# Moving the sequence-DFT stage of a gated FNet and feed-forward kernel between gate/up and the last feed-forward product, with the T sums of h made there

## The chip, the core and the metric

The kernel runs on one core of one Trainium2 chip, in fp32 results. The metric is the device time of one execution in microseconds (us): the kernel before takes 1018.36 us, the median of 3 runs between 1018.31 and 1018.51 us. Five engines work side by side and wait for each other through semaphores: TensorE (PE, matrix products), VectorE (DVE), ScalarE (ACT), GpSimd (POOL) and SyncE (SP). In this kernel POOL and SP do nothing but issue DMAs, SP mostly loads and POOL mostly stores. Each engine takes its instructions in the order in which they stand in its queue.

## What is computed

With S = 2048, D = 640 and F = 1728 the reference is, cut to what matters:

```
g = sigmoid((x * gate_w).sum(-1))                       # one gate per row
a = x @ dft_hid_re.T ;  b = x @ dft_hid_im.T
A = dft_seq_re @ a - dft_seq_im @ b                     # real part of a 2-D DFT
B = (gelu(x @ w_gate) * (x @ w_up)) @ w_down            # feed-forward
out = g * A + (1 - g) * B
```

The kernel takes the sequence DFT first (u = dft_seq @ x for the real and the imaginary matrix) and the hidden DFT after it, on the result.

## The kernel before, in words

**Precision.** Each fp32 operand is split into a high and a low part (`split`: `high` is a copy on ACT, `low` a subtraction on DVE), and each product is three PE instructions (`mm3`, lines 101 to 103). A product is one weight block of 128x128 against 512 columns.

**Seven products for eight.** All stages work on 2x2 blocks with seven products and sums of blocks. The sums of the left factor are called S, those of the right factor T.

**The stages, in the order of the program.**

1. *Gate/up*, a loop over 13 blocks of F (f = 0 to 12). It makes h = gelu(gate) * up in pairs of blocks. `keep` stores h's four blocks of a pair to DRAM (`hA[tp][k]`) and also four sums of them (`hT[tp][k]`), tp = 0, 1 being the halves of the rows and k = 0 to 5 the pairs. Small work that PE doesn't wait for (sums of weights, splits of the next operands) is put into a list, `fills`, from which some is taken after each product.
2. *Down*, 28 steps of `kseq`: h times w_down, from `hA`/`hT` and from w_down with its sums (`wsd`, made by `sum_wd` in gate/up). A step loads three steps ahead (`load_k`) and splits two steps ahead (`split_k`). The rows of h's first block, which F leaves over, have sums of their own (`hL`, by `sum_h0` and `sum_h0_narrow`). The result, times 1 - g, goes to `out`.
3. *C*, 64 steps of `cseq`: blocks of the sequence DFT's two matrices (`ct`, re and im, two halves j) times blocks of x. Eight steps with b = 0 (five pairs of products, 30 PE instructions; result banks X, Z, V, L, two each) and eight with b = 1 (four pairs, 24 instructions; banks Q, R, Y and again X) make one round; there are four rounds. In step i SP loads the DFT blocks of step i + 3 (tiles `cra`, `crb`, 512 KB each), and DVE and ACT split those of step i + 2 (`split_c`; for b = 1 DVE first makes four sums, `csa` and `csb`). x's own blocks are loaded, summed and split in the first steps (`fetch_xn`, `split_xa`, `split_xb`; some of it in the down stage) and stay in SBUF. At the end of b = 0 the eight banks are copied out so that b = 1 gets six of them; at the end of b = 1 the results are stored (`uA`) with their T sums (`uT`).
4. *U*, 20 steps of `useq`: u times the hidden DFT's matrices, times g, added onto `out` by accumulating DMAs. Its weights' sums (`wsu`) are made by `sum_wu` in the C stage.

The logits of the gate (ten of sixteen in gate/up, six in down) are a multiply-and-reduce on DVE of a loaded tile `xz` with the gate weights (`load_z`).

**What sets the order.** ACT and DVE run in the order in which the code issues their work (`in_order`). A scheduler orders SP's and POOL's DMAs and PE's products when the program is built. Large tiles come from one pool of 46 buffers of 512 KB (`slot`), 256 KB tiles from a pool of 14 (`mtile`), and weight pieces of 128 KB from a pool of 6 (`wsmall`); a load waits until the tile that had its buffer is done with.

The C stage's split has one special place, which both kernels have. In the last step of b = 0 (`held`), X is copied out first, then the DFT blocks of step i + 2 are split, and only then Z and L are copied out, all on ACT:

```
            for d in range(2):
                mm3(X[d], A(0, d), B[0], fst, lst)
            if held:
                for d in range(2):
                    sv["c11", d] = copy(X[d], f"s1{n}{d}")
                prepare()
```

Of the kernel before, what the change touches and what calls it, by code (L numbers as in the profile page):

```python
# [14 lines left out]
P = 128  # L15
# [10 lines left out]
XN_LOAD, XN_AT = [1, 5, 18, 22], [3, 7, 21, 24]  # L26
# [4 lines left out]
ZE_AT = [6, 8]  # L31
XB_DOWN = [17, 18]
XB_AT = [1, 3, 4, 5, 9, 10]
WU_AT = [4, 17, 19, 33, 35]
# [3 lines left out]
def kernel(  # L38
# [36 lines left out]
    def mtile(dt, name):  # L75
        return pool.tile([P, T], dt, tag="m", name=name, bufs=14)
# [157 lines left out]
    late_work, left_work, left_out = [], [], []  # L234

    def spare():
        for _, do in left_work:
            do()
        left_work.clear()
# [24 lines left out]
    def make_w(f):  # L264
# [96 lines left out]
        if kind == 1:  # L361
            if f > PAIRED:
                work = [(0, high_a), (0, neg_a), (84, across), (0, low_a), (56, across2), (0, high_q)]
                work += [(84, sums), (109, low_q), (84, sums2), (0, high_c), (56, diff_high), (0, spare), (0, diff_low), (122, low_c)]
# [88 lines left out]
    hid, todo = {}, deque()  # L453
# [74 lines left out]
    def gate_up(f, W, B, tp, s5, s1t, xs, s4):  # L528
# [69 lines left out]
        if not second:  # L598
            tt(s5, s2, s1, op=ALU.subtract)
            keep(hT[tp][k], 0, s5)  # L600
            hid[tp] = s2, s5
            yield
        h12, t1 = hid.pop(tp)

        def last_sums():
            tt(h12, s2, h12, op=ALU.subtract)  # L606
            keep(hT[tp][k], 2, h12)
            tt(t1, s2, t1, op=ALU.subtract)
            keep(hT[tp][k], 1, t1)

        def last_sum():
            tt(s5, s1, t1, op=ALU.subtract)
            keep(hT[tp][k], 3, s5)

        todo.extend([(122, last_sums), (61, last_sum)])
# [17 lines left out]
    def sum_wd(k):  # L633

        work = []

        def load():
            r, a21 = slot(F32, [P, 8, P], f"dr{k}"), wsmall(F32, f"da{k}")
            nc.sync.dma_start(r, wd[k, :, :8])
            nc.sync.dma_start(a21, wd[k, :, 8:])  # L640
            work.extend(do for _, do in sums_left(nc.sync, r[:, 0:2], r[:, 2:4], r[:, 6:8], a21, wsd[k]))

        def do():
            work.pop(0)()

        return [(0, load), (84, do), (84, do)]
# [20 lines left out]
    def sum_h0_narrow(tp):  # L667
# [13 lines left out]
        def second():  # L681
            tt(b21, b21, d2, op=ALU.add)
            left_out.append((hL[tp][:, 1], b21))

        return [(122, first), (61, second)]

    LEFT_AT = {2: lambda: [*sum_h0(0), *sum_h0(1)], 6: partial(sum_h0_narrow, 0), 12: partial(sum_h0_narrow, 1)}
# [74 lines left out]
    def split_xa(sp):  # L762
# [7 lines left out]
        sums_made.append(partial(split, h, l, r))  # L770
# [77 lines left out]

    def split_pieces(i):

        n = "{}{}{}".format(*kseq[i])
        r, raw = kraw.pop(i)
        names = ("A11", "A12", "e5", "S4")
        assert not kseq[i][1]
        B, W = [], {}

        def weights():
            h, l = slot(F32R, [P, 8, P], f"kh{n}"), slot(F32R, [P, 8, P], f"kl{n}")
            split(h, l, r)
            W.update({name: (at((h, l), 2 * q), at((h, l), 2 * q + 1)) for q, name in enumerate(names)})  # L860

        def right(q):
            v = hl(f"kb{n}{q}")
            split(*v, raw[q])
            B.extend([at(v, 0), at(v, 1)])

        ktile[i] = W, B
        return [(122, weights), (122, lambda: right(0)), (122, lambda: right(1))]
# [400 lines left out]
    with in_order(PE, ACT, DVE, POOL):  # L1269
        for f in range(1, NF):  # L1270
# [9 lines left out]
            if kind == 1:  # L1280
                lw, *w = sum_wd((f - PAIRED) // 2)
                if f == PAIRED:
                    lw[1]()
                    fills.extend(w)
# [3 lines left out]
            if f == NF - 1:  # L1288
                lw, *w = sum_wd(NK - 1)
                lw[1]()  # L1290
                fills.extend(w)
# [498 lines left out]
```

## Time and profile before

| | before |
|---|---|
| median of 3 runs | 1018.36 us |
| the profiled execution's own time | 1018.28 us |
| its span, first to last instruction | 1016.5 us |
| PE busy | 1012.4 us, 4489 instructions |
| DVE busy | 828.5 us (82%) |
| ACT busy | 486.0 us (48%) |
| POOL busy | 165.7 us (16%) |
| bytes moved by DMA | 265.74 MB, mean 261 GB/s |

Busy shares are averages over the stages. From the profile's timeline the stages lie at about 0 to 330 us (gate/up), 330 to 497 us (down), 497 to 890 us (C) and 890 us to the end (U). In the rows of the profile an instruction is named by line, engine, operation and its tiles, written before read.

### The profile page before, as it was taken

The page shows a single profiled execution, that of the slowest core. Times are in us where ns is not written, and L with a number is a line of the kernel's source. Part 1 is how long each engine was busy: PE and PEld are TensorE (multiplying, and loading weights), DVE is VectorE, ACT ScalarE, POOL GpSimd, SP SyncE. Part 2 cuts the span into 40 slices and gives each one's busy share as a digit, 9 for nine tenths or more (in the row PEclk, how much of TensorE's full clock was granted, in tenths as well). Part 3 has the DMA queues.
Part 4 walks back from the last instruction along what each step waited for, and adds up shares of the span by engine and source line. Part 5 has one row for each costly group of instructions (what it writes and reads, how often), then busy time and mean ns, then how long its engine had stood idle before and what let it go on. Part 6 is the DMA issues. An engine that isn't in the chain of part 4 may idle for free.

```text
span 1016.5 us, 13263 instructions
## 1 busy us (share of the span) xinstructions
PE 1012.4 (100%) x4489; PEld 836.4 (82%) x4489; DVE 828.5 (82%) x1164; ACT 486.0 (48%) x622; POOL 165.7 (16%) x295
## 2 busy tenths in 40 slices
PE   9999999999999999999999999999999999999998
PEld 7888888888888888888888888888888888888887
DVE  8887887977687989889888985888488869797796
ACT  6644434354545657457444443434344344455340
POOL 0221232323221200100001022102210200021112
PEclk9999999999999999999999999999999999999999
DMA  8557587968689999978865678658866868897856
GB/s 313 158 199 259 197 275 236 303 224 285 198 304 313 405 374 388 340 258 294 303 255 179 211 241 325 223 195 295 302 203 207 303 249 275 297 341 224 268 144 95
DMA packets 95988, 265.74 MB, mean 261 GB/s; under 512 B 12656, under 2 KB 26864, under 8 KB 95920
## 3 DMA queue, kind: packets, MB, share of 16 engines
q1 hardware_dynamic: 70368, 185.24, 53.4%
q0 software_dynamic: 25264, 79.46, 23.4%
q8 instruction: 35, 0.57, 0.2%
q14 instruction: 33, 0.27, 0.1%
q10 hardware_dynamic: 288, 0.20, 0.1%
HBM read 192.48 MB, written 70.27 MB: 258 GB/s over the span
## 4 chain that ended last, share of the span: by engine, by line
PE 99%; DMA 0%; ACT 0%; DVE 0%; ACTq 0%; issue 0%
PE pX L101 7%; PE pX L102 7%; PE pX L103 7%; PE pZ L101 5%; PE pZ L102 5%; PE pZ L103 5%; PE pL L102 3%; PE pL L101 3%; PE pL L103 3%; PE pV L102 2%; PE pV L101 2%; PE pV L103 2%; PE pQ L101 1%; PE pY L102 1%; PE pY L101 1%; PE pR L101 1%
## 5 line engine op out<-in xcount | busy, mean ns | idle before, releaser
L82 ACT ACTIVATE ch<-csa 128x1024 fp32r<-128x1024 f32 x32 | 34.0, 1063 | 79.0 <-DVE csa L797 77.6
L85 DVE TENSOR_TENSOR cl<-cra,ch 128x1024 fp32r<-128x1024 f32 x32 | 39.1, 1221 | 26.8 <-ACT ch L82 24.7
L82 ACT ACTIVATE ch<-cra 128x1024 fp32r<-128x1024 f32 x32 | 33.9, 1059 | 52.0 <-DVE cl L85 15.7
L85 DVE TENSOR_TENSOR cl<-crb,ch 128x1024 fp32r<-128x1024 f32 x32 | 39.1, 1221 | 14.3 <-ACT ch L82 14.3
L102 PE MATMUL pL<-cl,xah 128*128 128x512 f32 x128 | 49.8, 389 | 0.0
L103 PE MATMUL pL<-ch,xal 128*128 128x512 f32 x128 | 49.8, 389 | 0.0
L101 PE MATMUL pL<-ch,xah 128*128 128x512 f32 x128 | 49.6, 389 | 0.0
L422 POOL DMA_DIRECT2D hA<-s x48 | 26.1, 545 | 138.8 <-DVE s L589 119.3
L82 ACT ACTIVATE ch<-crb 128x1024 fp32r<-128x1024 f32 x32 | 33.8, 1056 | 29.6 <-PE pL L102 11.6
L85 DVE TENSOR_TENSOR cl<-csb,ch 128x1024 fp32r<-128x1024 f32 x32 | 39.2, 1224 | 3.7 <-ACT ch L82 2.3
L85 DVE TENSOR_TENSOR cl<-csa,ch 128x1024 fp32r<-128x1024 f32 x32 | 39.1, 1220 | 2.1 <-ACT ch L82 1.1
L82 ACT ACTIVATE ch<-csb 128x1024 fp32r<-128x1024 f32 x32 | 34.0, 1062 | 11.7 <-DVE csb L800 5.3
L148 ACT ACTIVATE s<-pX 128x512 f32<-128x512 f32 x41 | 24.3, 596 | 28.9 <-PE pX L103 28.4
L583 ACT ACTIVATE s<-s 128x512 f32<-128x512 f32 x24 | 15.2, 633 | 45.6 <-DVE s L582 45.6
L82 ACT ACTIVATE kh<-kw 128x1024 fp32r<-128x1024 f32 x24 | 25.5, 1063 | 15.6 <-DMA kw<-wsd 6.4
L578 DVE TENSOR_TENSOR s<-s,pX 128x512 f32<-128x512 f32 x24 | 16.4, 684 | 20.0 <-PE pX L103 20.0
L1437 POOL DMA_DIRECT2D uA<-c x8 | 4.3, 540 | 168.9 <-DVE c L1539 168.6
L85 DVE TENSOR_TENSOR kl<-kw,kh 128x1024 fp32r<-128x1024 f32 x24 | 29.2, 1217 | 1.9 <-ACT kh L82 1.0
L422 POOL DMA_DIRECT2D hT<-s x48 | 25.9, 540 | 18.6 <-DVE s L606 7.4
L959 POOL DMA_DIRECT2D out<-ks x12 | 6.5, 541 | 136.4 <-DVE ks L958 135.8
L564 ACT ACTIVATE s<-pZ 128x512 f32<-128x512 f32 x24 | 14.2, 595 | 29.4 <-PE pZ L103 24.1
L101 PEld LDWEIGHTS pL<-ch,xah 128*128 128x128 f32 x128 | 24.0, 188 | 5.0
(3655 smaller groups left out, 3484.8 us busy)
## 6 DMA issues: line engine op xcount, KB each, us to landing
cra<-in_ct SPq DMA_DIRECT2D x64, 512.0 KB, 4.3
crb<-in_ct SPq DMA_DIRECT2D x64, 512.0 KB, 4.9
hA<-s POOLq DMA_DIRECT2D x48, 256.0 KB, 5.5
hT<-s POOLq DMA_DIRECT2D x48, 256.0 KB, 5.0
kr<-hA SPq DMA_DIRECT2D x24, 512.0 KB, 7.3
kr<-hT SPq DMA_DIRECT2D x24, 512.0 KB, 6.9
ux<-uA SPq DMA_DIRECT2D x24, 512.0 KB, 5.9
ux<-uT SPq DMA_DIRECT2D x16, 512.0 KB, 6.6
```

The costliest lines, as they stand in the source:

```text
L82: nc.scalar.activation(hi, raw, AF.Copy)
L85: nc.vector.tensor_tensor(lo, raw, hi.bitcast(F32), op=ALU.subtract)
L101: nc.tensor.matmul(ps, lh, rh, start=first, stop=False, skip_group_check=True)
L102: nc.tensor.matmul(ps, lh, rl, start=False, stop=False, skip_group_check=True)
L103: nc.tensor.matmul(ps, ll, rh, start=False, stop=last, skip_group_check=True)
L148: nc.scalar.activation(m, src, AF.Copy)
L422: nc.gpsimd.dma_start(to[:, i], src)
L564: nc.scalar.activation(s5, Z, AF.Copy)
L578: tt(s5, s5, X, op=ALU.add)
L583: nc.scalar.activation(s2, s2, AF.Gelu_apprx_tanh)
L959: nc.gpsimd.dma_start(acc4[:, t] if tp and e == 4 else out[2 * tp + t, e], src)
L1437: nc.gpsimd.dma_start(to[:, i], src)
```

## The change

The C stage is moved from behind the down stage to behind gate/up; the down stage then stands between C and U. With it:

- h's T sums are no longer made in gate/up from h's tiles in SBUF. `sum_h(tp, k)` loads the four blocks of `hA[tp][k]` again (four loads of 256 KB), makes the four sums on DVE and stores them (four stores of 256 KB). It runs twelve times in the second to fourth rounds of the C stage: at steps 18, 19, 20 and 29 of the first of them (counted from the start of C), and 16 and 32 steps later.
- the sums of w_down (`sum_wd`) are made at steps 18 and 20 of these rounds, two a round, and stored from POOL's queue instead of SP's.
- ten logits are made in the C stage (`ZC_AT`), loaded in the step named and summed in the next.
- x's blocks, which were loaded and split in down and in C's first steps, are now loaded and split in gate/up's last block and C's first eight steps; six of the eight low parts come from an accumulating DMA instead of DVE (`by_dma`).
- of the five sums of the hidden DFT's weights, three stay in C at other steps and two move into down.
- `sum_h0_narrow` moves into down, the load of the hidden DFT's weights from C's last round to the seam between down and U, the sigmoid of the first gate half from gate/up to the start of down; `mtile` gets 15 buffers for 14.

The diff, cut to its core:

```
-XN_LOAD, XN_AT = [1, 5, 18, 22], [3, 7, 21, 24]
-XB_DOWN = [17, 18]
-XB_AT = [1, 3, 4, 5, 9, 10]
-WU_AT = [4, 17, 19, 33, 35]
+XB_AT = [0, 1, 2, 3, 4, 5, 6, 7]
+WU_AT, WU_DOWN = [18, 34, 50], [10, 17]
...
-        return pool.tile([P, T], dt, tag="m", name=name, bufs=14)
+        return pool.tile([P, T], dt, tag="m", name=name, bufs=15)
...
-        if not second:
-            tt(s5, s2, s1, op=ALU.subtract)
-            keep(hT[tp][k], 0, s5)
-            hid[tp] = s2, s5
-            yield
...
-        todo.extend([(122, last_sums), (61, last_sum)])
         yield
...
+        r, a21 = slot(F32, [P, 8, P], f"dr{k}"), wsmall(F32, f"da{k}")
+        nc.sync.dma_start(r, wd[k, :, :8])
+        nc.sync.dma_start(a21, wd[k, :, 8:])
+        return [do for _, do in sums_left(nc.gpsimd, r[:, 0:2], r[:, 2:4], r[:, 6:8], a21, wsd[k])]
+
+    def sum_h(tp, k):
+        b11, b12, b21, b22 = (mtile(F32, f"ht{tp}{k}{q}") for q in range(4))
+        for q, v in enumerate((b11, b12, b21, b22)):
+            nc.sync.dma_start(v, hA[tp][k][:, q])
...
+            tt(b11, b12, b11, op=ALU.subtract)
+            keep(hT[tp][k], 0, b11)
+            tt(b12, b22, b12, op=ALU.subtract)
+            keep(hT[tp][k], 2, b12)
+            tt(b22, b22, b11, op=ALU.subtract)
+            keep(hT[tp][k], 1, b22)
+            tt(b21, b21, b22, op=ALU.subtract)
+            keep(hT[tp][k], 3, b21)
...
+        def by_dma():
+            high(h, r)
+            negative(l, r)
+            left_of(l, r)
...
+    HT_AT, WD_AT, ZC_AT = {}, {}, [17, 22, 30, 33, 38, 46, 49, 53, 54, 62]
+    for g in range(3):
+        for q, r in enumerate((2, 3, 4, 13)):
+            HT_AT[16 * g + 16 + r] = q % 2, 2 * g + q // 2
+        for q in range(2):
+            WD_AT[16 * g + 18 + 2 * q] = 2 * g + q
...
+        ready, units = units, []
+        if i in HT_AT:
+            units += sum_h(*HT_AT[i])
+        if i in WD_AT:
+            units += sum_wd(WD_AT[i])
+        if i in ZC_AT:
+            (_, first), (_, total) = load_z(1)
+            first()
+            units.append(total)
...
         held = not b and sp == NP - 1
         if not held:
             prepare()
+        for do in ready:
+            do()
```

How the queues change at the seam from b = 0 to b = 1 of the second round (steps 22 to 26; the first number in a name, as in `cra24`, is the step). SP's queue, the loads of steps 23 to 26, before:

```order
L788 DMA cra23_5651<-in_ct 128x1024
L788 DMA crb23_5652<-in_ct 128x1024
L788 DMA cra24_5700<-in_ct 128x1024
L788 DMA crb24_5701<-in_ct 128x1024
L788 DMA cra25_5750<-in_ct 128x1024
L788 DMA crb25_5751<-in_ct 128x1024
L788 DMA cra26_5798<-in_ct 128x1024
L788 DMA crb26_5799<-in_ct 128x1024
```

and in the changed kernel, from the last load of an h block (`ht`) on; `dr` and `da` are the pieces of w_down for `sum_wd`, `ua` one for `sum_wu`, `xz` the tile of a logit:

```order
L620 DMA ht013_3982<-hA01_66 128x512
L611 DMA dr1_3987<-in_wd 128x1024
L612 DMA da4_5571<-in_wd 128x256
L777 DMA cra24_4037<-in_ct 128x1024
L777 DMA crb24_4038<-in_ct 128x1024
L686 DMA ua2_5585<-in_wu 128x256
L777 DMA cra25_4095<-in_ct 128x1024
L777 DMA crb25_4096<-in_ct 128x1024
L726 DMA xz1_4099<-in_xz 128x640
L612 DMA da5_5705<-in_wd 128x256
L777 DMA cra26_4145<-in_ct 128x1024
L777 DMA crb26_4146<-in_ct 128x1024
```

Between the DFT loads now stand other loads, among them `da4` and `da5`, which belong to the fourth round (steps 50 and 52): the scheduler put them here, and each takes a buffer of the pool of six that an earlier `da` has until its sums are stored.

DVE's queue in the held step 23, from the last low part of step 24 on, before:

```order
L85 TENSOR_TENSOR cl24_1_5765<-csb24_5757,ch24_1_5764 128x1024
L796 TENSOR_TENSOR csa25_5812<-cra25_5750 128x512
L797 TENSOR_TENSOR csa25_5812<-crb25_5751,cra25_5750 128x512
L799 TENSOR_TENSOR csb25_5815<-crb25_5751,csa25_5812 128x512
L800 TENSOR_TENSOR csb25_5815<-csb25_5815,crb25_5751 128x512
```

and in the changed kernel:

```order
L83 TENSOR_TENSOR cl24_1_4112<-csb24_4104,ch24_1_4111 128x1024
L730 ISA xz1_4099,z_63<-xz1_4099,gwb_64 128x640
L730 ISA z_63 128x1
L785 TENSOR_TENSOR csa25_4160<-cra25_4095 128x512
L786 TENSOR_TENSOR csa25_4160<-crb25_4096,cra25_4095 128x512
L788 TENSOR_TENSOR csb25_4163<-crb25_4096,csa25_4160 128x512
L789 TENSOR_TENSOR csb25_4163<-csb25_4163,crb25_4096 128x512
```

The logit's reduction, which needs the load of `xz1`, moved ahead of step 25's four sums. ACT's queue at this place has the same work in the same order in both kernels; in the changed one it reads (`s1` are the copies of X, `s3` those of Z):

```order
L146 ACTIVATE s1010_4156<-pX010_3758 128x512
L146 ACTIVATE s1011_4158<-pX011_3759 128x512
L80 ACTIVATE ch25_0_4166<-csa25_4160 128x1024
L80 ACTIVATE ch25_1_4170<-csb25_4163 128x1024
L146 ACTIVATE s3010_4198<-pZ010_3760 128x512
L146 ACTIVATE s3011_4200<-pZ011_3761 128x512
```

The copies of Z stand behind the high parts of step 25, which read the sums of DVE above.

More of the change, by code (lines that the diff above doesn't have):

```diff
@@ L232, in load_up @@
         return r
[L234 to L239, printed above, removed]
+    late_work, left_out = [], []
     def make_up(f, r):
@@ L1317 @@
             store_left()
[L1318 to L1325 removed]
+            if f == 2:
+                k = len(fills) // 2
+                rest = [fills.pop() for _ in range(len(fills) - k)]
+                fills.extend([*sum_h0(0), *sum_h0(1), *reversed(rest)])
+                state["all"] = sum(c for c, _ in fills)
             for _ in range(4):
@@ L1594 @@
         if after:
-            after.pop(0)()
+            late() if i == 0 else after.pop(0)()
         if i < ND:
             load_uw(1, i)
+            if i < 2:
+                split_uw(0, ND - 2 + i)
+            split_uw(1, i)
         fst, lst = p == 0, p == ND - 1
```

191 lines of the change are left out of this document (71 added, 120 removed).

## The prediction

> **What bounds the kernel now.** I read the page first: span, busy times, the DMA slices and the chain that ended last.
>
> ```profile
> span 1016.5 us, 13263 instructions
> ...
> PE 1012.4 (100%) x4489; PEld 836.4 (82%) x4489; DVE 828.5 (82%) x1164; ACT 486.0 (48%) x622; POOL 165.7 (16%) x295
> ...
> GB/s 313 158 199 259 197 275 236 303 224 285 198 304 313 405 374 388 340 258 294 303 255 179 211 241 325 223 195 295 302 203 207 303 249 275 297 341 224 268 144 95
> ...
> PE 99%; DMA 0%; ACT 0%; DVE 0%; ACTq 0%; issue 0%
> ```
>
> PE is busy for all but 4.1 us of the span (1016.5 - 1012.4), and the chain is PE alone. Next, PE's waits, the whole answer:
>
> ```profile
> PE idle L1059 <- PEq L1778: 0.8, 1, 0.8
> PE pg L101 <- ACT w0h L82: 0.2, 1, 0.2
> ```
>
> After the start PE never waits, so nothing that is taken off DVE, ACT or a queue can shorten the run. Since a matmul's record overlaps the next one's, I take its pace from starts: the first product of step 23 of the C stage and that of step 24.
>
> ```profile
> 644.55 0.39 PE L101 MATMUL pX<-ch,xah 128*128 128x512 f32 x1
> ...
> 651.35 0.39 PE L101 MATMUL pX<-ch,xbh 128*128 128x512 f32 x1
> ```
>
> 6.80 us for 30 instructions is 0.2267 us each, with no gap to close. The change issues the same number of matmuls on the same shapes, with the start and the end of the program as they were. So PE's 1012.4 us stay, and the question is only whether PE begins to wait. I therefore looked at what feeds it, stage by stage (columns: busy us of PE, its weight loads, DVE, ACT and POOL; granted clock, DMA share, GB/s).
>
> ```profile
> 25.00:330.00 305.00, 305.00 (x1345) 252.04 (x1344) 244.89 (x434) 144.12 (x227) 77.61 (x141) 1.00 0.74 246
> ...
> 597.30:651.30 54.00, 54.00 (x240) 44.72 (x239) 39.31 (x52) 20.80 (x27) 13.23 (x25) 1.00 0.80 279
> ```
>
> Gate/up (first row) has a full PE, so DVE's freed time gains nothing there. The second row is the eight b = 0 steps of C's second round, steps 16 to 23. They already have the DMA engines busy for 0.80 of the time, right where the change puts most of its transfers.
>
> **The change part by part.**
>
> *Gate/up gives up* 48 sums on DVE, here two of their four groups, with a sum of 256 columns below them:
>
> ```profile
> L599 DVE TENSOR_TENSOR s<-s,s 128x512 f32<-128x512 f32 x12 | 8.3, 692 | 0.4
> ...
> L606 DVE TENSOR_TENSOR s<-s,s 128x512 f32<-128x512 f32 x12 | 8.2, 683 | 0.0
> ...
> L768 DVE TENSOR_TENSOR xm<-xm 128x256 f32<-128x256 f32 x8 | 3.4, 425 | 0.3
> ```
>
> With the other two groups of twelve that is 33 us of DVE, the 48 stores of POOL, the w_down sums and ten logits. All of it lay beside a PE that was never idle: gain 0.
>
> *C's rounds two to four take it over.* Three of a round's four `sum_h` and both `sum_wd` fall into the eight b = 0 steps. Sizes of the transfers:
>
> ```profile
> hT<-s POOLq DMA_DIRECT2D x48, 256.0 KB, 5.0
> ...
> xz<-in_xz SPq DMA_DIRECT2D x16, 320.0 KB, 5.4
> dr<-in_wd SPq DMA_DIRECT2D x6, 512.0 KB, 6.1
> ur<-in_wu SPq DMA_DIRECT2D x10, 256.0 KB, 6.5
> wsd<-dr SPq DMA_DIRECT2D x18, 128.0 KB, 1.8
> wsu<-ur POOLq DMA_DIRECT2D x15, 128.0 KB, 3.5
> wneg<-ur POOLq DMA_DIRECT2D x6, 256.0 KB, 6.4
> ```
>
> Bytes of these steps before: 279 GB/s for 54.0 us, 15.07 MB. Out go the two `sum_wu` that stood at steps 17 and 19: twice three loads and four stores (0.655 + 0.524 MB) and one `wneg` of two stores (0.524), 2.88 MB. In come one `sum_wu` (1.18), three `sum_h` of four loads and four stores of 256 KB each (24 x 0.262 = 6.29), two `sum_wd` (2 x 1.18 = 2.36), two logit tiles (0.66), and two early small loads, `da4` and `ua2` (0.26): 22.9 MB. Over eight steps (8 x 6.80 = 54.4 us) that is 421 GB/s. What can the engines carry? Stretches where they were full:
>
> ```profile
> 606.00:622.00 16.00, 16.00 (x72) 13.25 (x71) 11.68 (x16) 3.44 (x4) 6.49 (x12) 1.00 1.03 378
> ...
> 807.00:813.00 6.00, 6.00 (x29) 4.95 (x28) 3.12 (x3) 1.38 (x2) 0.54 (x1) 1.00 1.03 418
> ...
> 334.00:406.00 72.00, 72.00 (x326) 59.10 (x325) 66.99 (x80) 47.61 (x54) 6.68 (x13) 1.00 1.02 389
> ...
> 384.00:396.00 12.00, 12.00 (x55) 9.94 (x54) 12.00 (x15) 10.34 (x11) 2.18 (x4) 1.00 1.03 404
> ```
>
> With a share of 1.02 to 1.04 the rate is 378 to 418 GB/s. The first row is the nearest case: the same stage, the start of the same round, with loads and stores mixed. I take 378; the other end is 418. So **these eight steps ask for more than the channel carries**, and a lag builds up.
>
> *Where the lag reaches PE.* Step 23 is the held step: Z's copies on ACT stand behind step 25's high parts, these behind DVE's four sums for step 25, and these now stand behind the logit's reduction, whose tile SP loads behind all else. The first product into Q waits for ACT. Before, at this place:
>
> ```profile
> 645.43 1.28 ACT L148 ACTIVATE s<-pX 128x512 f32<-128x512 f32 x2 [3.92 <-PE pX L103]
> 646.61 1.05 ACT L82 ACTIVATE ch<-csa 128x1024 fp32r<-128x1024 f32 x1
> 647.55 1.05 ACT L82 ACTIVATE ch<-csb 128x1024 fp32r<-128x1024 f32 x1
> 648.50 1.07 ACT L148 ACTIVATE s<-pZ 128x512 f32<-128x512 f32 x2
> ```
>
> ```profile
> 641.59 1.22 DVE L85 TENSOR_TENSOR cl<-csb,ch 128x1024 fp32r<-128x1024 f32 x1
> 644.53 0.69 DVE L796 TENSOR_TENSOR csa<-cra 128x512 f32<-128x512 f32 x1 [1.72 <-PE pL L102]
> ```
>
> From DVE's first sum (644.53) to the end of the first Z copy (648.50 + 0.6) are 4.57 us. The logit itself and its landing:
>
> ```profile
> L747 DVE CUSTOM_DVE_ANT_0 xz<-xz,gwb x16: 810/816/819, 148.6 to 438.5; 128x640 f32<-128x640 f32 x16
> ...
> DMA to landing us min/median/max: 3.6/5.4/8.8
> ```
>
> ```profile
> L747 DVE DVE_READ_ACCUMULATOR2_ANT z<- 128x1 f32 x16 | 1.3, 80 | 0.0
> ```
>
> Of the 22.9 MB, step 26's DFT blocks (1.05) and about 1.0 of stores come after the logit tile, so 20.9 MB go first: 55.3 us at 378 GB/s, counted from the start of step 16. The shortest landing, 3.6 us, less the tile's own transfer leaves 2.7 us behind the last byte. The tile is there at 55.3 + 2.7 - 54.4 = 3.6 us after step 24 should begin. Then 0.82 + 0.08 on DVE and 4.57 to the copy: 9.1 us. PE has six instructions of step 24 (X, 1.36 us) and then waits: **7.7 us**. At 404 GB/s the same sum gives 4.1, at 418 2.4. Rounds three and four repeat it (logits at steps 38 and 54): 3 x 7.7 = 23.1 us.
>
> *DVE* in the eight steps: 39.3 us busy before, plus 12 sums of h at 0.69, eight of w_down at 0.42 (256 columns), two logits at 0.9, less one `sum_wu` (1.7): 51.0 of 54.4 us. It is just hidden. Its lead was 8.5 us (641.59 + 1.22 against 651.35), and it has only 3.4 us in hand if loads make it idle.
>
> *The seams.* Gate/up's last block gets two splits of x and of DFT blocks (each three sums of 256 columns, 1.27 us, and three low parts of 1.22, in all 9.9) for three low parts (3.7): 6 us more of DVE beside 17.7 us of PE (78 matmuls). Before, PE waited there 0; bounds 0 and 2, I take 1. From C to down, the last round's stores meet the loads of three steps; before, the same stores met U's loads with no wait: bounds 0 and 3, I take 1. C's first eight steps carry five more x loads, the accumulating DMAs and no `sum_h`; bounds 0 and 2, I take 0, for less is asked of the channel than above. Down to U, the moved gate, `sum_h0_narrow` and `mtile`'s fifteenth buffer: 0, between -0.5 and 2; they lie beside products and the down stage loses x's work.
>
> Sum against the profiled execution's own 1018.28 us (span 1016.5 and 1.8 around it; 0.08 under the median): 1018.28 + 23.1 + 2 = **1043 us**.
>
> *A rule of the Trainium skill.* The rows above put a full channel at 378 to 418 GB/s. "DMA: Bandwidth & Descriptors", section "Where 436 GB/s comes from", names 435 GB/s as the ceiling of the ports and says that for transfers between HBM and SBUF the HBM side, about 358, binds. By 435 the wait would be 0.4 us a round and the time 1021; by 358 it would be 10.8 and the time 1053. This trace agrees with neither: 389 over 72 us is above the one, and no full stretch that I read reaches the other.
>
> **The rivals.**
>
> *The channel carries more (1025 to 1036).* At 418 GB/s, 3 x 2.4 = 7.2 us: 1025 without the seams; at 404, 12.3 and 2: 1033. For it: two of the four rows are above 400. Against it: the nearest row is the lowest, and the 418 lasted 6 us. (By the skill's 435 the far end is 1021.)
>
> *Not slower (1018 to 1020).* The lag vanishes before step 24 if the logit's tile is early enough: 47.6 us for 20.9 MB (54.4 + 1.36 - 2.7 - 5.5), so 439 GB/s, or 18.0 MB at 378. The mechanism is prefetch: if SP gets buffers early, some eleven of the 24 transfers of h leave the crowded steps. For it: 20% of those steps is idle channel today, and step 24's low parts had 8.5 us to spare. Against it: each `ht` load waits for a buffer of the pool of fifteen, which the end of a round fills.
>
> *SP held up by `da` and `ua` loads (1052 to 1062).* `da4` stands ahead of step 24's blocks and waits until an earlier `da` was summed and stored by POOL. If that store takes the longest landing of anything on `hT`, loads among them (12.1 us, below), rather than the 5.0 of its stores, the queue runs dry for up to 7.1 us; half of it in three rounds is 10.6 us: 1054. DVE with 3.4 us in hand couldn't make it up.
>
> ```profile
> L422 POOL DMA_DIRECT2D hT<-s x48: 539/539/548, 68.7 to 346.1; - x48
> ...
> DMA to landing us min/median/max: 2.4/6.0/12.1
> ```
>
> **How the numbers follow.** Forecast (1036 to 1052): 0.46. More channel (1020.4 to 1036): 0.22. SP held up (over 1052): 0.19. Not slower: 0.12, and 0.01 that PE's idle 4.1 us shrink by half. The range 1022 to 1058 leaves out the case of no change and the far ends of both, some 0.19. About 0.2%, 2 us, is what a measurement of this kernel can tell from no change. Faster 0.01, same 0.11, slower 0.88.
>
> **What would show it.** PE's waits in the profile after: three of 4 to 9 us, on the first product into Q at steps 24, 40 and 56, released by ACT; ACT's high parts there idle for DVE's sums, and the logit's reduction idle for its load. DMA share about 1.0 from step 16 to 24 of rounds two to four, near 378 GB/s. Gate/up's DVE about 50 us lighter and PE's busy time unchanged. It would be wrong if the share stays under 0.95 there, if the waits come at steps 18 to 22 instead (DVE the bound), or if PE waits mostly at a seam.

## The result, and the profile after

| | before | changed |
|---|---|---|
| median | 1018.39 us (4 runs, 1018.31 to 1018.51) | 1059.86 us (4 runs, 1057.12 to 1063.71) |
| ratio, 95% interval | | 1.041 (1.037 to 1.045) |
| the profiled execution's own time, span | 1018.28, 1016.5 us | 1058.28, 1056.5 us |

The changed kernel is slower by 41.5 us; 25 were forecast, and the time lies 1.9 us above the range. First the page of the changed kernel:

```profile
span 1056.5 us, 13360 instructions
...
PE 1024.0 (97%) x4489; PEld 839.9 (79%) x4489; DVE 823.8 (78%) x1158; ACT 487.9 (46%) x625; POOL 185.0 (18%) x327
...
PE 62%; issue 16%; DMA 16%; DVE 3%; POOL 2%; ACT 0%; SPq 0%; POOLq 0%; DVEq 0%
```

The chain was PE alone; now it runs through DMAs and queues. PE's busy time rose by 11.6 us at an unchanged number of products, so waits alone are not the whole story. PE's waits (us in total, times, longest):

```profile
PE pQ L99 <- ACT s L146: 13.9, 2, 7.4
PE pX L99 <- ACT ch L80: 6.3, 2, 6.0
PE pX L99 <- ACT s L146: 3.4, 3, 1.5
PE pX L101 <- DMA xal<-xn: 2.3, 2, 1.6
PE pX L100 <- DVE cl L83: 1.4, 4, 0.5
...
PE kZ L99 <- DVE ksa L985: 0.7, 1, 0.7
PE pL L99 <- DVE sa L1469: 0.5, 2, 0.2
```

But for 0.2 us at step 8, the first three lines are waits at steps 24, 40 and 56: 23.4 us. The three long ones, of the kind that was forecast, are 7.4, 6.5 and 6.0, 19.9 us together; in the other 3.4 us (third line) the first product of these steps waits for the copy of X. Next, the b = 0 and b = 1 halves of rounds two to four, each window from the first product of a half to that of the next (busy us of PE, weight loads, DVE, ACT, POOL; granted clock, DMA share, GB/s):

```profile
434.71:490.63 55.92, 54.57 (x241) 44.86 (x240) 42.85 (x62) 15.59 (x17) 20.01 (x37) 1.00 1.00 351
490.63:544.31 53.68, 45.99 (x193) 37.35 (x193) 43.44 (x55) 22.95 (x27) 4.87 (x9) 0.94 0.78 261
544.31:600.95 56.64, 54.86 (x241) 44.78 (x240) 45.07 (x65) 15.78 (x17) 20.54 (x38) 1.00 1.00 371
600.95:653.60 52.65, 45.91 (x193) 37.30 (x194) 43.18 (x55) 22.50 (x27) 4.32 (x8) 0.90 0.72 251
653.60:709.25 55.65, 54.86 (x242) 44.78 (x240) 44.98 (x65) 17.42 (x22) 21.45 (x40) 1.00 1.02 384
709.25:762.08 52.83, 46.52 (x192) 37.74 (x193) 48.91 (x63) 24.66 (x29) 4.49 (x9) 0.94 0.92 339
```

At the prediction's pace of 0.2267 us a round of 432 instructions takes 97.9 us. Here the three take 109.6, 109.3 and 108.5: 11.7, 11.4 and 10.6 us lost, **33.7** in all. The spans differ by 40.0, so 6.3 us lie elsewhere: 4.2 in C's first round, 1.1 in the down stage, the rest scattered. The b = 0 halves have a full channel (the core's 16 DMA engines together; share 1.00 to 1.02) at 351 to 384 GB/s. Most of the loss sits at the start of the b = 1 halves, and there the mean clock is below 1. The first of these places, on DVE, ACT and PE:

```profile
490.63 0.50 PE L99 MATMUL pX<-ch,xbh 128*128 128x512 f32 x1 [1.35 <-ACT s L146]
...
495.26 0.83 DVE L730 CUSTOM_DVE_ANT_0 xz<-xz,gwb 128x640 f32<-128x640 f32 x1 [3.91 <-DMA xz<-in_xz]
496.01 0.69 DVE L785 TENSOR_TENSOR csa<-cra 128x512 f32<-128x512 f32 x1
497.42 1.06 ACT L80 ACTIVATE ch<-csa 128x1024 fp32r<-128x1024 f32 x1 [6.35 <-DVE csa L786]
499.62 1.07 ACT L146 ACTIVATE s<-pZ 128x512 f32<-128x512 f32 x2
500.25 0.80 PE L99 MATMUL pQ<-ch,xbh 128*128 128x512 f32 x1 [7.42 <-ACT s L146]
```

It is the forecast's chain: logit's tile, reduction, sums, high part, Z's copy, and a wait of 7.42 us (7.7 forecast). What PE then does is seen in the clock (the column after POOL) around it:

```profile
488.00:493.00 5.00, 3.21 (x12) 1.78 (x10) 3.27 (x4) 2.74 (x4) 1.22 (x3) 1.00 1.02 391
493.00:497.00 4.00, 0.00 (x0) 0.00 (x0) 1.74 (x4) 0.00 (x0) 0.00 (x0) 1.00 0.38 137
497.00:498.00 1.00, 0.00 (x0) 0.00 (x0) 0.96 (x3) 0.58 (x1) 0.00 (x0) 0.58 0.95 283
...
500.00:503.00 3.00, 2.75 (x7) 2.17 (x8) 3.00 (x5) 1.66 (x4) 1.30 (x3) 0.50 0.99 356
...
504.00:506.00 2.00, 2.00 (x11) 1.60 (x9) 1.81 (x2) 1.38 (x2) 0.00 (x0) 1.00 0.72 169
```

The clock falls to half during the wait and stays there for 3.7 us after PE resumed: 7 products in 3 us, where 11 take 2 us later. And SP's queue ahead of this place, with what it waited for between 434 and 762 us:

```profile
467.01 0.33 SPq L611 DMA_DIRECT2D dr<-in_wd  x1
477.45 0.33 SPq L612 DMA_DIRECT2D da<-in_wd  x1
477.87 0.38 SPq L777 DMA_DIRECT2D cra<-in_ct  x1
478.67 0.33 SPq L777 DMA_DIRECT2D crb<-in_ct  x1
...
481.64 0.49 SPq L726 DMA_DIRECT2D xz<-in_xz  x1
495.44 0.33 SPq L612 DMA_DIRECT2D da<-in_wd  x1
```

```profile
SPq L612 <- DMA wsd<-da: 23.3, 2, 13.3
...
SPq L777 <- DMA wsd<-dr: 10.3, 2, 10.0
```

```profile
xz<-in_xz SPq DMA_DIRECT2D x16, 320.0 KB, 9.1
...
wsd<-dr POOLq DMA_DIRECT2D x18, 128.0 KB, 6.9
```

SP stood for 10 us with `da4` and later for 13 us with `da5`, until the store of an earlier `da` had landed; the second of these lines is mostly a DFT load in the next round, which stood 10.0 us for a store of `dr` (issued at 604.49 us). The last two lines are DMA issues with their median from issue to landing: 6.9 us for these stores (1.8 before), 9.1 for a logit's tile (5.4 before). The tile issued at 481.64 was reduced at 495.26.

### The profile page after: what moved, and what is told of

Read it like the earlier page. It is cut to its first block, busy times and chain, and to the rows that moved or that the text cites. A ratio compares the mean times of both kernels' runs of the same rounds, so it can differ in the third digit from the quotient of the medians.

```text
span 1056.5 us, 13360 instructions
## 1 busy us (share of the span) xinstructions
PE 1024.0 (97%) x4489; PEld 839.9 (79%) x4489; DVE 823.8 (78%) x1158; ACT 487.9 (46%) x625; POOL 185.0 (18%) x327
## 4 chain that ended last, share of the span: by engine, by line
PE 62%; issue 16%; DMA 16%; DVE 3%; POOL 2%; ACT 0%; SPq 0%; POOLq 0%; DVEq 0%
DMA ht<-hA 4%; PE pX L99 4%; PE pX L101 4%; PE pX L100 4%; DMA xz<-in_xz 4%; PE pZ L101 3%; PE pZ L100 3%; PE pZ L99 3%; DMA cra<-in_ct 2%; DMA crb<-in_ct 1%; DMA uA<-s 1%; PE kX L99 1%; PE kX L101 1%; PE kX L100 1%; PE kL L100 1%
## 5 line engine op out<-in xcount | busy, mean ns | idle before, releaser
L80 ACT ACTIVATE ch<-csa 128x1024 fp32r<-128x1024 f32 x32 | 34.0, 1062 | 123.8 <-DVE csa L786 102.0
L415 POOL DMA_DIRECT2D hT<-ht x48 | 26.0, 541 | 144.4 <-DVE ht L623 134.6
L80 ACT ACTIVATE ch<-crb 128x1024 fp32r<-128x1024 f32 x32 | 33.8, 1057 | 25.0 <-PE pL L100 10.3
L99 PE MATMUL pQ<-ch,xbh 128*128 128x512 f32 x64 | 26.7, 417 | 13.9 <-ACT s L146 13.9
L576 ACT ACTIVATE s<-s 128x512 f32<-128x512 f32 x24 | 15.1, 633 | 46.8 <-DVE s L575 46.8
L99 PE MATMUL pX<-ch,xbh 128*128 128x512 f32 x64 | 25.6, 406 | 9.7 <-ACT ch L80 6.3
```

The source lines that it names most:

```text
L80: nc.scalar.activation(hi, raw, AF.Copy)
L99: nc.tensor.matmul(ps, lh, rh, start=first, stop=False, skip_group_check=True)
L415: nc.gpsimd.dma_start(to[:, i], src)
L576: nc.scalar.activation(s2, s2, AF.Gelu_apprx_tanh)
```

## The experiments

All kernels are the changed one with one or more edits, but for the last two, which are the kernel before. "Lost" is what a round takes beyond 97.9 us, in the profiled execution; "elsewhere" is the span less 1016.5 us and less these three.

| run | median us | lost in rounds 2, 3, 4 | elsewhere |
|---|---|---|---|
| changed kernel | 1059.86 | 11.7, 11.4, 10.6 | 6.3 |
| e1 h in gate/up | 1044.72 | 6.4, 6.8, 0.0 | 11.4 |
| e10 w_down in gate/up | 1039.21 | 0.5, 6.0, 10.3 | 5.0 |
| e11 both | 1028.62 | 0.0, 0.0, 0.0 | 10.4 |
| e16 both, x by DVE | 1025.06 | 0.0, 0.0, 0.0 | 5.9 |
| e14 buffers free | 1051.75 | 6.3, 9.8, 8.7 | 9.7 |
| e3 logits later | 1051.59 | 8.5, 8.2, 8.6 | 5.6 |
| e15 e14 and e3 | 1040.84 | 4.7, 3.5, 7.9 | 7.1 |
| e18 e15, h not loaded | 1029.12 | 1.0, 0.7, 0.7 | 7.6 |
| e5 h not loaded | 1045.29 | 9.5, 7.6, 0.0 | 11.3 |
| e4 h not summed | 1072.70 | 21.8, 15.1, 12.0 | 8.0 |
| e2 loads by code | 1063.86 | 12.2, 11.2, 15.0 | 5.6 |
| e6 x by DVE | 1057.20 | 12.3, 10.9, 11.1 | 5.8 |
| e13 four rounds | 1062.09 | 13.0, 7.8, 1.5 | 21.3 |
| e19 mended | 1037.03 | 0.2, 6.4, 7.9 | 4.4 |
| f1 before, 9 operations | 1033.01 | 0.6, 0.6, 6.2 | 7.5 |
| f2 before, 14 operations | 1050.53 | 6.6, 5.6, 10.4 | 9.7 |

**Which part of the work costs.** e1 puts h's T sums back into gate/up, e10 w_down's sums:

```
         keep(hA[tp][k], 2 * second, s1)
+        if not second:
+            tt(s5, s2, s1, op=ALU.subtract)
+            keep(hT[tp][k], 0, s5)
...
-            HT_AT[16 * g + 16 + r] = q % 2, 2 * g + q // 2
```

```
+            if kind == 1 or f == NF - 1:
+                fills.extend(sum_wd((f - PAIRED) // 2 if kind == 1 else NK - 1))
...
-            WD_AT[16 * g + 18 + 2 * q] = 2 * g + q
```

e11 has both edits.

> One part undone: h's T sums are made in gate/up from the tiles in SBUF, as before the change; the stage order and all else of the change stay. The theory of a full channel: the first eight steps of a round lose 3 x 2.10 of 22.9 MB and ask for 16.6 MB in 54.4 us, 305 GB/s, well under the 368 GB/s that the changed kernel's channel carried when full. So nothing lags, the three waits of 6 to 8 us at the end of b = 0 vanish, and with them every row of half clock; what stays is 5 us of small waits at C's start and at the seams: 1022 to 1027 us. The theory that SyncE's queue is what holds the DFT blocks back (the loads of da and ua that the scheduler put ahead of them): the three da loads of later rounds are still in front, so waits of 2 to 4 us stay in each round: 1030 to 1045 us. The theory of DVE as the bound: 12 sums of 0.69 us less in each round, 8.3 us, and no wait: as the first, so this run does not tell those two apart.

> One part undone: the sums of w_down are made and stored in gate/up, as before the change; h's T sums stay in the C stage. The b = 0 halves then ask for 22.9 - 2.36 - 0.13 = 20.4 MB, 375 GB/s, about what the channel carried when full (368 from 440 to 493 us of the changed kernel), and no DFT tile takes a buffer that a store still reads. Held buffers: the three large waits go, apart from rests of 0 to 2 us where the full channel lets a DFT block come late: 1022 to 1032 us. Full channel alone, by the forecast's own sum: the logit's tile has 18.4 MB ahead of it, 50 us at 368 GB/s, and is in time as well: 1022 to 1028 us. A third theory, that h's loads and stores are what costs, whatever else is there: half of the loss or more stays, 1038 to 1050 us.

> Two parts undone: h's T sums and the sums of w_down are both made in gate/up, as before; the order of the stages, x's blocks, the ten logits and the sums of the hidden DFT's weights stay as in the changed kernel. If what the C stage got to carry is the whole price, only the small waits of C's start (4 us with the low parts of x by accumulating DMA) and of the seams stay: 1021 to 1026 us. If the order of the stages itself costs, by its seams or by the logits, it stays above 1030 us.

With both gone from C the three rounds lose nothing, so the whole 33.7 us come from these two jobs; the order of the stages has no part in them. Each alone leaves about half (13.2 and 16.8). The pure channel theory fell with e1: its first b = 0 half has a channel no fuller than before (0.81 and 281 GB/s from 440 to 494 us), and still PE lost 6.4 us. DVE's row in e1 says why:

```profile
478.78 0.43 DVE L620 TENSOR_TENSOR dr<-dr 128x256 f32<-128x256 f32 x1
487.00 0.69 DVE L803 TENSOR_TENSOR csa<-cra 128x512 f32<-128x512 f32 x1 [7.80 <-DMA wsd<-dr]
```

The tile `csa` of step 24 takes the buffer of `dr1`, and may only be written when the last store of w_down's sums has landed. The forecast didn't have such a wait: `dr` was summed 8 us earlier. Who gets the buffer differs by kernel. In the changed kernel it was loads, for which SP stood (the rows of its queue above), and not step 25's sums, as the expectation of e3 below supposes.

**Held buffers, and the logit.** e14 makes w_down's sums but doesn't store them; its stores, of the same size, write another tile, so that `dr` and `da` are free once summed. e3 moves three logits:

```
+                if free:
+                    v = gwb[:, : 2 * P].rearrange("p (a b) -> p a b", a=2)
                 engine.dma_start(to[:, 2 * i : 2 * i + 2], v)
```

```
-    HT_AT, WD_AT, ZC_AT = {}, {}, [17, 22, 30, 33, 38, 46, 49, 53, 54, 62]
+    HT_AT, WD_AT, ZC_AT = {}, {}, [17, 26, 30, 33, 42, 46, 49, 53, 58, 62]
```

> Left out: the sums of w_down are made but not stored; the 24 stores to wsd write a part of the gate weights' tile gwb instead, from the same queue, at the same place, of the same size. So bytes, loads, sums and the number of stores are those of the changed kernel, but the buffers of dr and da are free when DVE has summed, and not only when the stores have landed. The theory of held buffers: in the changed kernel SyncE stood from 467.0 to 477.4 us until the store of da0 had landed (issued at 469.9), then the load of crb24 until a store of dr0 landed, and csa56 in the last round waited for the stores of dr4 itself. Without these the DFT blocks and the logit's tile are issued up to 10 us earlier and at least half of the 32 us of the three rounds goes: 1022 to 1042 us. The theory of a full channel: the same 22.9 MB have to pass in each b = 0 half, so the logit's tile and step 25's sums are as late as before: 1050 to 1060 us.

> One thing is moved: the logits of steps 22, 38 and 54 are loaded four steps later, so that no logit's reduction stands ahead of DVE's sums for the step after the held one. The forecast's own chain (the reduction waits for its tile, and step 25's sums for the reduction): 3 to 4 us a round go and the half clock with them, 1040 to 1052 us. The theory of held buffers: in the changed kernel the last store of dr1 landed at 495.57 us, 0.4 us ahead of step 25's first sum, and the loads behind SyncE's wait are as late as before; taking away the logit's tile saves its own 0.33 MB, about 1 us a round: 1055 to 1061 us.

> Left out, as in the run with free buffers: the sums of w_down are made but not stored, the stores write a part of the gate weights' tile. And the logits of steps 22, 38 and 54 are loaded four steps later. Each alone took 8 us off (1051.75 and 1051.59 from 1059.86). If both are in one chain, one behind the other (a late logit behind a held queue), the gains add or overlap: 1042 to 1048 us, and what stays are the DFT blocks themselves, landing late in a full channel. If each hid behind the other, so that only both together free the place, most of the rest goes as well: 1025 to 1036 us.

Each takes 8 us off the median, both together 19. So they are links of one chain, and neither is the whole of it: held buffers didn't bring the half that their theory asked for, and the logit brought the low end of what the forecast's chain asked for. In e14, with free buffers, the logit's tile is still what DVE waits for:

```profile
489.11 0.82 DVE L732 CUSTOM_DVE_ANT_0 xz<-xz,gwb 128x640 f32<-128x640 f32 x1 [1.78 <-DMA xz<-in_xz]
```

**Bytes, or DVE.** e4 drops the sums of h and keeps all transfers; e5 drops the loads and keeps sums and stores:

```
-            tt(b11, b12, b11, op=ALU.subtract)
-            keep(hT[tp][k], 0, b11)
...
+            for q, v in enumerate((b11, b22, b12, b21)):
+                keep(hT[tp][k], q, v)
```

```
-            nc.sync.dma_start(v, hA[tp][k][:, q])
...
-            tt(b11, b12, b11, op=ALU.subtract)
+            tt(b11, gwb[:, :T], gwb[:, :T], op=ALU.subtract)
```

e18 is e15 with e5's edit.

> Left out: the four DVE sums of each of the twelve pairs of h's blocks; the blocks are loaded and stored as they are, with the same loads, stores and bytes. The theory of DVE as the bound: 12 x 0.69 = 8.3 us less on DVE in the first eight steps of each round, so the waits of 6 to 8 us vanish: 1025 to 1035 us. The theory of a full channel: the bytes are the same, so the waits stay; stores may be issued some us earlier, which moves bytes ahead of the logit's tile rather than behind it: 1055 to 1062 us.

> Left out: the loads of h's blocks for the T sums; DVE makes its 48 sums from the gate weights' tile instead, and POOL stores them as before. So 3.15 MB of loads leave the b = 0 half of each round (22.9 to 19.8 MB, 363 GB/s), while the 48 stores, the work of DVE and the sums of w_down stay. Theory: a full channel and held buffers both cost, and freeing the channel of half of h's bytes brings most of what leaving h out altogether brought (1044.7 us): 1045 to 1052 us. Rival, that it is the stores that cost, since POOL's stores of w_down's sums stand behind h's in the same queue and SyncE and DVE wait for their landing: 1053 to 1060 us. By the forecast's own sum the logit's tile would be in time with 19.8 MB and all waits would go: 1022 to 1030 us.

> Three things at once: the stores of w_down's sums write the gate weights' tile (the sums are made and not stored), the logits of steps 22, 38 and 54 are four steps later, and h's blocks aren't loaded (DVE's 48 sums are made from the gate weights' tile, their stores stay). With the first two 14 us were left in the three rounds (1040.8 us). If those 14 us are the DFT blocks themselves, landing late in a full channel, 3.15 MB less in each b = 0 half brings nearly all of it: 1024 to 1030 us, and the waits left are those of C's start (4 us) and of the down stage (2 to 5 us). If they come from DVE or from POOL's queue of stores, which are as long as before: 1034 to 1041 us.

With less of DVE's work e4 is slower by 13 us, more than any theory had. There POOL's queue waits for the landing of h's blocks, whose stores stand ahead of those of w_down; the latter are issued from 473.6 us on (468.7 in the changed kernel), and ACT waits 10 us for them:

```profile
484.20 1.06 ACT L80 ACTIVATE ch<-crb 128x1024 fp32r<-128x1024 f32 x1 [10.02 <-DMA wsd<-dr]
```

e5 came out at the fast end of its own theory, and 17.1 us of the three rounds' loss stay without h's loads. e18 closes the account: with free buffers, later logits and half of h's bytes, the three rounds lose 2.4 us, where e15 lost 16.1. DVE has all its sums there, so DVE as the bound is out. The difference is h's loads alone. No run parts their bytes from their place in SP's queue, but e15's channel was full without a break up to 2 us before its first wait in these rounds:

```profile
440.00:488.00 48.00, 48.00 (x214) 39.74 (x213) 36.93 (x52) 13.51 (x14) 13.57 (x25) 1.00 1.03 394
```

PE's waits in e18 have no long one in C any more:

```profile
PE kZ L99 <- DVE ksa L985: 2.4, 1, 2.4
PE pX L101 <- DMA xal<-xn: 2.1, 2, 1.4
PE pL L99 <- DVE sa L1469: 0.9, 2, 0.5
...
PE pQ L99 <- ACT s L146: 0.7, 1, 0.7
```

**The order in SP's queue.** e2 issues C's loads as the code gives them:

```
     sv, wus = {}, {}
+    loads = ExitStack()
+    loads.enter_context(in_order(SP))
```

> One thing is changed in the order alone: in the C stage SyncE's loads are issued as the code gives them, so da4, ua2 and da5 no longer stand ahead of the DFT blocks of steps 24 and 26. Bytes and sums are the same. The theory that SyncE's queue is held up: in the changed kernel SyncE issued nothing for 10 us after dr (467.0 to 477.4 us) and for 13 us after da4; without these the DFT blocks of step 24 come early, its X no longer waits, and at least half of the 32 us of the three rounds goes: 1028 to 1045 us. The theory of a full channel: the channel carried 368 GB/s with a share of 1.02 from 440 to 493 us all the same, so the same bytes have to pass before the logit's tile; only the 1.4 us that X of step 24 waits for its own blocks, and the 2 us in which the share fell to 0.85, can be had back, about 3 us a round and somewhat less half clock: 1045 to 1058 us.

A miss for both theories: 4 us slower than the changed kernel in the median (the ranges overlap a little). SP no longer stands with `da4`, but the end of the chain is the buffer itself:

```profile
492.56 0.83 DVE L730 CUSTOM_DVE_ANT_0 xz<-xz,gwb 128x640 f32<-128x640 f32 x1 [3.43 <-DMA xz<-in_xz]
...
495.62 0.69 DVE L785 TENSOR_TENSOR csa<-cra 128x512 f32<-128x512 f32 x1 [2.23 <-DMA wsd<-dr]
```

**C's first round.** e6 makes x's low parts on DVE; e16 is e11 with this edit.

```
-            split_xa(i + 2, False)
+            split_xa(i + 2)
```

> One part undone: the low parts of x's blocks in C's first round are made by DVE in one subtraction each, instead of a copy on ACT and an accumulating DMA of POOL (six of eight). The theory that the small waits of C's first round (2 us at 346 to 349, 2 us at 385 to 393 us, the first product with xah or xal of a step) come from the accumulating DMA, which lands late in a full channel: they go, 3 to 4 us: 1055 to 1057 us, and the three large waits are as they were. The rival, that DVE has no room there: six more subtractions of 1.22 us stand ahead of the sums and low parts of the DFT blocks and the waits move to those: 1059 to 1065 us.

> Three parts undone: h's T sums and w_down's sums in gate/up, as before the change, and the low parts of x's blocks by DVE instead of accumulating DMAs. The stage order, the logits, the hidden DFT's sums and the seams are those of the changed kernel. The run with the first two parts undone had 1028.6 us, with 8 of its 10 us in three places of C's first round, the longest a wait of 3.1 us for xal by DMA and 4 us of half clock behind it. If the accumulating DMAs are their cause, 7 to 8 us go: 1020 to 1022 us, and the order of the stages is free to within 2 us. If C's first round is late for its x loads instead: 1025 to 1029 us.

The waits for `xal` are gone in both, for 2.7 and 3.6 us of the median (e6 ranges from 1053.98 to 1059.0, so its gain is not sharp). e16 stays 6.4 us above the kernel before: one wait of 1.8 us for ACT's `ch` in C's first round, with half clock behind it, is the largest piece. The new order of the stages is nearly free, not free. e11 shows why the accumulating DMAs were late; the windows around its longest wait for `xal`:

```profile
355.00:357.00 2.00, 2.00 (x11) 1.65 (x10) 2.00 (x4) 1.65 (x2) 0.00 (x0) 1.00 1.07 391
358.00:361.00 3.00, 0.05 (x1) 0.06 (x1) 2.59 (x5) 2.35 (x4) 0.68 (x1) 1.00 1.03 209
```

The engines are full in both, at 391 and at 209 GB/s; in the second nearly all packets are POOL's.

**The price of a wait.** f1 and f2 add only DVE time to the kernel before, in `split_c`, and no byte:

```
+            if cseq[i][3] == 1:
+                for _ in range(14):
+                    tt(gwb[:, :T], gwb[:, :T], gwb[:, :T], op=ALU.max)
             s1 = pair(F32, f"csa{i}")
```

> The kernel before, with one thing added: nine DVE operations of 128x512 that change nothing (the larger of a value and itself) ahead of the four sums for the step after each held step, in all four rounds. No byte more is moved. Nine such dependent operations take about 9 x 0.73 = 6.6 us; DVE had been idle for 1.7 us there, and the first copy of Z stood 3.6 us ahead of the first product into Q (649.1 against 652.7 us in the profile of before), so PE waits some 1.2 us a round. If only the wait counts, or the wait is too short for the clock to fall (in the changed kernel waits of 1.4 to 1.6 us left the granted clock at 1.00): 4 x 1.2 = 5 us, 1021 to 1025 us, no row at half clock. If every wait costs clock: 2 us more a round, 1029 to 1033 us.

> As the run with nine operations, with fourteen: 14 x 0.73 = 10.2 us, a wait of some 4.9 us in each of the four rounds, with a DMA channel as little used as before. If the half clock follows from PE's wait alone, each round costs the wait and 1.6 to 3.1 us more (what the runs so far lost in slow products behind waits of 1.8 us and longer), and stretches of about 4 to 6 us with a granted clock of 0.50 follow each wait: 4 x 4.9 = 20 and 6 to 12 us more, 1044 to 1051 us. If the half clock comes from the full channel or another load of the changed kernel: 20 us only, 1036 to 1040 us, clock at 1.00.

The four waits came out uneven (f1: 4.0 and 4.1 us and two of none, where 1.2 each was expected; f2: 7.6, 3.7, 3.7 and 7.7), since DVE's lead differs by round: in f1 its nine operations ended 1.8 and 1.9 us after the start of the b = 1 half in rounds one and four, 2.1 us before it in the others. The rule is clear all the same. f2's waits are 22.7 us in all, its four rounds lose 32.0 (9.4 in the first): 9.3 us, 2.3 a wait, come on top, nearly all of it at half clock. f1's two rounds with a wait lose 7.1 and 6.2. f2 around its first wait, which ends at 562.84 us:

```profile
555.00:556.00 1.00, 0.23 (x2) 0.00 (x0) 0.97 (x2) 0.00 (x0) 0.00 (x0) 1.00 0.71 242
...
558.00:559.00 1.00, 0.00 (x0) 0.00 (x0) 0.97 (x2) 0.00 (x0) 0.00 (x0) 1.00 0.00 0
559.00:560.00 1.00, 0.00 (x0) 0.00 (x0) 1.00 (x3) 0.00 (x0) 0.00 (x0) 0.60 0.00 0
...
565.00:566.00 1.00, 1.00 (x3) 0.77 (x3) 1.00 (x3) 0.00 (x0) 0.88 (x3) 0.50 0.26 102
566.00:567.00 1.00, 1.00 (x6) 0.78 (x5) 1.00 (x2) 0.47 (x1) 0.93 (x2) 0.98 0.82 303
```

The clock fell and stayed at half while the channel moved nothing. So the half clock follows from the wait, not from the new load.

**Two repairs.** e13 spreads the work over all four rounds, moves the logits, and has the edits of e2 and e6; e19 keeps h's sums in C and mends the rest (the edits of e10, e3, e6 and e2 together).

```
+        for q, r in enumerate((6, 10, 13)):
+            HT_AT[16 * g + r] = (3 * g + q) % 2, (3 * g + q) // 2
+    for k, at_i in enumerate((8, 12, 24, 28, 40, 56)):
+        WD_AT[at_i] = k
```

> All of the change's work stays in the C stage, at other steps: h's twelve pairs three a round over all four rounds (steps 6, 10 and 13 of each), w_down's sums at steps 8, 12, 24, 28, 40 and 56, the logits away from the held steps, SyncE's loads in the order of the code, and the low parts of x by DVE. So the b = 0 half of a round gets one pair of h instead of three and at most one sum of w_down instead of two: 22.9 - 2 x 2.10 - 1.18 - 0.13 = 17.4 MB, 320 GB/s; the b = 1 half gets two pairs and one sum, some 17 MB in 43.5 us, 390 GB/s, more than before, but its steps have no held step in front of them. Theory of channel and buffers: the large waits at the end of b = 0 go, smaller ones may come at the end of b = 1: 1024 to 1036 us. Rival, that the work is too much for the C stage wherever it stands (some 35 MB a round in 97.9 us, 355 GB/s): 1040 to 1055 us.

> A version of the changed order that keeps h's T sums in the C stage and mends what the runs have shown to cost: w_down's sums in gate/up as before, the three logits four steps later, x's low parts by DVE, SyncE's loads in the order of the code. The parts alone: 1039.2 (w_down), 8 us for the logits, 3 us for x. Theory of a channel at its limit in the b = 0 halves: 20.4 - 0.3 MB, 369 GB/s, is just what it carries, so that rests of 0 to 3 us a round stay: 1022 to 1031 us. It cannot be faster than before, where PE had no wait: not under 1018 us. Rival, that h alone fills the channel too far for any order of loads: 1032 to 1040 us.

e13 gained nothing: its waits moved to the end of the b = 1 halves, 7.0 and 7.1 us on X at the start of rounds two and three, behind ACT's copy. That copy stands behind a high part, which waited for a buffer that a store of w_down's sums still read (4.6 us in the second case; the channel was full, share 1.01 from 424 to 436 us):

```profile
441.43 1.06 ACT L80 ACTIVATE ch<-crb 128x1024 fp32r<-128x1024 f32 x1 [4.52 <-DMA wsd<-dr]
```

So here too the stored tile holds the place up, whatever round it is in. e19 came out in its rival's range: h alone is enough to make rounds three and four late. No version beat the kernel before, whose PE has nothing to gain.

## Why the prediction was right in direction and mechanism, and wrong in size

- *Gate/up gains nothing:* right; with both jobs put back there (e11) PE waits 0.2 us at gate/up's end.
- *The b = 0 halves ask for more than the channel carries:* right. 378 GB/s were taken, 351 to 384 measured at full share (19.6 to 21.4 MB in these halves, where 22.9 were asked for), and by e18 h's loads alone are worth 13.7 us (16.1 less 2.4).
- *Where the lag reaches PE:* right as to place and number, three times, by ACT's Z copy behind DVE's sums; in the last round X waited instead, for step 57's high part. These three waits are 19.9 us, 23.1 were forecast; 3.4 us more are waits for X's copy, which stands on ACT behind step 24's own late high parts and which the forecast didn't have.
- *But the 7.7 us were worked out from the logit's tile alone.* Without it (e3) 25.3 of the 33.7 us stay, since DVE then waits for step 25's DFT blocks, and its second sum starts only 4.2 us earlier (492.41 us). And with buffers free (e14) the same chain waits 4.6 us in the second round, not 7.4: the channel alone gives less than the forecast had from its lowest rate, and the held buffers make up for it. That the size agreed is partly luck.
- *The step that failed* is "a wait costs its length". The term 3 x 7.7 counted the waits and let PE resume at 0.2267 us. The rounds lost 33.7 us, 10.3 beyond the waits at these three places. Of these, 1.3 are small waits (`cl`, `pL`) and about 6, 2 a round, are products at half clock: it lasted 3.7, 3.5 and 4.9 us after PE resumed, with products 0.43 us apart. The other 3 lie mostly at the edges of the eleven waits, since a product's record lasts 0.39 us and the idle time is counted from its end. f2 shows the price in isolation, 2.3 us a wait beyond its length. The Trainium skill has this in "TensorE: Matmul & The Clock Gate", section "What's actually happening": the clock is half or full, falls after an idle window of about 3.4 us and returns after about 3.4 us of work, in windows that run free. It should have been weighed: by it each of three 7.7 us waits is followed by up to 3.4 us at half pace, an estimate of up to 1.7 us each. The traces agree on the two levels; the clock stayed low for 3.2 to 5.6 us behind f2's waits, somewhat longer than the Trainium skill has it, and it fell in shorter gaps (last section).
- *C's first eight steps, taken as 0:* wrong, 2.9 us in these steps and 1.3 in the rest of the round. Fewer bytes were asked for (227 GB/s), but the accumulating DMAs occupy the channel at half its rate (e11's rows), and PE waits for `xal`. The other seams, taken as 2, came to about 2.
- *The rival "SP held up" (1052 to 1062, chance 0.19)* holds the measured time. Its mechanism was there, 10 and 13 us on `da`, but it is not the cause by itself: with SP in code order (e2) nothing was gained, since the buffers are held whoever waits for them. Free buffers are worth 8 us. Its price was misread besides: 12.1 us is the longest landing on `hA`, on `hT` it is 10.3, by which the rival's own sum gives 1051.
- *DVE just hidden:* hidden, but not just: it was busy for 42.9 to 45.1 us in these halves, where 51.0 were forecast. e4 took work from it and won nothing.

In numbers: 1018.28 + 33.7 + 6.3 = 1058.3 for the profiled execution, against 1018.28 + 23.1 + 2. Of the 15 us between, 10.6 lie in the three rounds: about 6 at half clock, 4.7 in waits for X's copy and small waits, 3 at the waits' edges, less 3.2 by which the three long waits were shorter. The other 4.3 are nearly all C's first round.

## What to carry to other kernels

On an engine that never waits, a wait costs more than its length: add what the clock takes behind it, in f1 and f2 1.8 to 3.1 us for each wait of 3.7 us or more. When work is moved into a stage, count not only its bytes against the channel but how long its buffers stay taken: a tile that is stored is free when the store lands, in a full channel 7 us later, and whoever gets that buffer next waits, in whatever queue. And where several things end within a few microseconds of each other, taking away the one that ended last shows only the next.

## What the hardware showed that was not expected

- The granted clock fell in waits well under 3.4 us too, and where a wait lies counts as much as its length. In all the traces here the clock changes on a fixed grid of 3.41 us: each stretch at half clock, but for the one that the end of the run cuts off, lasts 3.41 us or a multiple of it (497.15 to 503.98 us in the changed kernel, 602.97 to 613.21, 715.61 to 722.43). A stretch of this grid at full clock in which PE idled for 1.85 us or more was always followed by half clock, one with less than 1.68 us never; in between both occur. Two stretches each of e6 and of e18, in the down stage:

```profile
843.35:846.76 3.41, 1.56 (x8) 0.99 (x7) 3.41 (x6) 2.51 (x3) 0.00 (x0) 1.00 1.03 407
846.76:850.17 3.41, 3.41 (x9) 2.67 (x10) 3.41 (x7) 1.15 (x2) 0.00 (x0) 0.50 1.04 414
...
813.70:817.11 3.41, 1.90 (x9) 1.24 (x7) 3.41 (x5) 2.99 (x3) 0.40 (x1) 1.00 1.04 416
817.11:820.52 3.41, 2.52 (x11) 1.93 (x12) 3.41 (x7) 1.17 (x2) 0.00 (x0) 1.00 1.04 412
```

e6's wait of 1.85 us lies in one stretch and cost the next one its clock. e18's wait of 2.40 us is the longer one, but it is split 1.5 to 0.9, and no slow products followed. In the changed kernel a wait of 1.54 us and a small one were enough together (at 602.97 us, 0.2 us before the long wait of that place began).

- A full channel is not one rate: 351 to 384 GB/s in C's b = 0 halves with loads and stores mixed, 391 to 416 GB/s in short stretches above, 209 GB/s with accumulating DMAs on the way.
